# A fused attention and mixture-of-experts kernel: the last tile's outputs normalised on ScalarE, three low parts moved one step, the job table read elsewhere

## The chip, the core and the metric

The kernel runs on one core of a Trainium2 chip. The metric is device time in microseconds (us), the median of several executions; lower is better. Durations of single instructions come from one profiled execution.

## The reference, cut to what matters

```python
B, H, S, D = 8, 8, 576, 64                    # batch, heads, sequence, head size
k_p, v_p = k.reshape(B, H, 72, 8, D).mean(3), v.reshape(B, H, 72, 8, D).mean(3)
scores = (1 / np.sqrt(D)) * np.matmul(q, k_p.transpose(0, 1, 3, 2))
attn = np.exp(scores - scores.max(-1, keepdims=True))
attn = attn / (attn.sum(-1, keepdims=True) + 1e-9)
x = np.matmul(attn, v_p).transpose(0, 2, 1, 3).reshape(4608, 512)
logits = x @ w_gate                           # 8 experts
e_idx = logits.argmax(1)
probs = softmax(logits)
eom = 1 / (1 + np.exp(-(x @ w_output_gate)))
for e in range(8):                            # each row goes to one expert
    mask = e_idx == e
    h = np.maximum(x[mask] @ w1[e], 0)        # 512 -> 1024
    out[mask] = gate_w[mask, None] * eom[mask, e, None] * (h @ w2[e])
```

## The kernel before, in words

The program has two stages with a barrier between them (the profile puts the barrier down to L1716, the line that opens the first stage's scheduling context).

**Stage one** is `attention_and_routing`, written as one order of instructions per engine; each engine follows its own order and waits on semaphores. It walks over 36 tiles of 128 rows in a software pipeline: at step i, in two halves a = 0 and 1, it computes the scores of tile i (`scores`, L279), the peak (`peak`, L285, VectorE), the exponentials (`softmax`, L291, ScalarE), the transposes of tile i-2 (`transpose_p`, L304) and the output of tile i-3 (`values`, L313: matmuls; L330: VectorE's reciprocals of the row sums into `grec`). `normalise` (L333 to L338) then multiplies the unnormalised outputs, 3 heads in half 0 and 5 heads in half 1, by those reciprocals: one VectorE `tensor_tensor` per half (L336) that reads PSUM and writes `xg` in a layout where the 8 heads lie side by side, so that neighbouring elements of one head are 8 floats apart. Each head has 80 columns: 16 gate logits and 64 outputs. The last tile is i = 35; its two PSUM tiles are named `av`.

`route(g)` is a generator that routes four tiles at a time: L352 (`lg`, the sum of the gate logits over heads, which needs all heads of the four tiles), then a chain of small VectorE operations (mx L356, d L358, cand L362, best L364, oh L366), two exponentials on ScalarE (ex L359, ez L373), the rank matmuls (`rk`, L376 and L378) on the matmul engine PE, and the destination `where` (L401), with which GpSimd scatters the rows to DRAM (L447). After the last group, `closing` and `job_table` (L414 to L437, L705 to L735) count the rows of each expert and write `table`, ten integers.

The first expert's first 384 rows are taken early: `turn_x` (L483) transposes them on VectorE (part 0, L486), rounds them to the high part on ScalarE (part 1, L488) and takes the low part on VectorE (part 2, L490), at steps that `TURNS` lists for the three row blocks.

After the loop over tiles a hand-written string `TAIL` orders the rest. Each letter calls `first_layer`: M is a chunk of the first layer (L669, 12 matmuls; the first M has two chunks, 24 matmuls, and takes all products with high parts first), H its ReLU on ScalarE (L525), L its low part on VectorE (L529), a, A the splitting of weights on ScalarE (L475), d, D that on VectorE (L479), W n takes n pieces from the queue of routing generators, R computes slot rows on VectorE (L692 to L702), Y is three matmuls of the second layer (L675), and T makes each of the five engines read the ten integers of `table` into registers (L516, `TENSOR_LOAD`). Below, L0 to L7 are the eight low parts and D0 to D3 the four split pieces of VectorE in this order.

**Stage two** is `experts`: every engine loops over experts by the register values of the job table, with semaphores written out by hand. PE first runs the remaining 33 second-layer matmuls of the first block (L675), then the next products (L1105, L1130).

Of the kernel before, what the change touches and what calls it, by code (L numbers as in the profile page):

```python
# [15 lines left out]
AF = mybir.ActivationFunctionType  # L16
# [4 lines left out]
B, H, S, D = 8, 8, 576, 64  # L21
KEYS, POOL = 72, 8
N, DM, FF, E = B * S, H * D, 1024, 8
P = 128
NT = N // P
# [5 lines left out]
R = 56  # L31
# [5 lines left out]
GATE = 2 * E  # L37
LEAD = GATE * H
# [7 lines left out]
HEADS = (3, 5)  # L46
# [11 lines left out]

TAIL = 'M a W9 d H L W3 M A H L W6 D M A H L W6 D M A H L W6 D M A H L W12 D M H L R M H L T Y Y Y Y Y H L'.split()
F0 = TAIL.count('Y')

AHEAD = {3: 8, 2: 8}
# [1 line left out]
INIT = 5  # L66
POS = (4, 6)
BEHIND = 2
TURNS = ((35.5, 36, 36), (36, 37, 37), (37, 37, 37))
AHEAD_OF_X = 8  # L70
HALF = 512
PARITY = 29120
# [22 lines left out]
def attention_and_routing(ctx, tc, sh, qT, kT, v, wg, wst, xs):  # L95
    nc = tc.nc
# [174 lines left out]
    s_t, pT_t, xg, grec = {}, {}, {}, {}  # L271
# [34 lines left out]
    def values(i, a):  # L306
        av = sh.p_y[a] if i < NT - 1 else ps_t.tile([P, 512], F32, tag="t", name=f"av{a}")
        pT = pT_t[i]
        slot = 4 * a
        for c in chunks(a):  # L310
            _, h, n_heads = CHUNKS[c]
            for r0, n, b, s0 in segments(i):
                nc.tensor.matmul(av[r0:r0 + n, COLS * h:COLS * (h + n_heads)], pT[:, c, r0:r0 + n],  # L313
                                 vbd[b % 2][:, slot:slot + n_heads].rearrange("p h f -> p (h f)"),
                                 start=(c == chunks(a)[0]), stop=(c == chunks(a)[-1]), skip_group_check=True)
            slot += n_heads
        g, j = place[i]
        if a == 0:
            if j == 0:
                while len(placed) < sum(GROUPS[:max(g - 2, 0)]):  # L320
                    work(1, True)
                    place_ids()
                xg[g] = p2.tile([P, GMAX, LEAD + ROW], F32, tag="xg", name=f"xg{g}", bufs=3)
                n, t0 = group(g)
                nc.gpsimd.iota(xg[g][:, 0:n, LEAD + ID:], pattern=[[P, n], [0, ROW - ID]], base=t0 * P, channel_multiplier=1,
                               allow_small_or_imprecise_dtypes=True)
                grec[g] = p2.tile([P, GMAX, H], F32, tag="grec", name=f"grec{g}")
        hs = slice(3 * a, 3 + 5 * a)
        avv = av[:, 0:HEADS[a] * COLS].rearrange("p (h f) -> p h f", h=HEADS[a])
        nc.vector.reciprocal(grec[g][:, j, hs], avv[:, :, COLS - 1])  # L330
        return avv

    def normalise(i, a, avv):  # L333
        g, j = place[i]
        hs = slice(3 * a, 3 + 5 * a)
        nc.vector.tensor_tensor(xg[g][:, j, 0:LEAD + DM].rearrange("p (f h) -> p f h", h=H)[:, :, hs],  # L336
                                avv[:, :, 0:GATE + D].rearrange("p h f -> p f h"),
                                grec[g][:, j, hs].unsqueeze(1).to_broadcast([P, GATE + D, HEADS[a]]), op=ALU.mult)  # L338
# [134 lines left out]
    def split_hi(c, whole=0):  # L473
        m, h, src, hi, lo = early(c, whole)
        nc.scalar.activation(hi, src, AF.Copy)  # L475

    def split_lo(c, whole=0):
        m, h, src, hi, lo = early(c, whole)
        nc.vector.tensor_tensor(lo, src, hi.bitcast(F32), op=ALU.subtract)  # L479
        if h and m + STAGES < LOADED:  # L480
            stage_in(m + STAGES)
# [12 lines left out]
    def first_layer(kind):  # L494
        if kind == "M":
            accs = {}
            for _ in range(1 if layered else 2):
                f = len(layered)
                accs[f] = (sh.p_h + sh.p_y[1:])[f % 4][:, 0:WIDE * P]
                layered.append(accs[f])  # L500
            hidden_chunks(nc, sh, accs)
        elif kind == "Y":
            outputs.append(output_chunk(nc, sh, len(outputs), sh.p_y[0], 0))
        elif kind == "a":
            split_hi(AHEAD_OF_X - 1)
        elif kind == "d":
            split_lo(AHEAD_OF_X - 1)
        elif kind == "A":
            split_piece.append(len(split_piece))
            split_hi(2 * 4 + split_piece[-1], 1)  # L510
        elif kind == "D":
            split_lo(2 * 4 + split_done.pop(), 1)
        elif kind == "T":
            assert not queue
            for eng in (nc.tensor, nc.scalar, nc.vector, nc.gpsimd, nc.sync):
                sh.loaded[eng.engine] = nc.values_load_multi_w_load_instructions(  # L516
                    sh.table[0:1, 0:E + 2], [eng.engine], min_val=0, max_val=1023,
                    skip_runtime_bounds_check_because="counts of a few bits each")[1]
        elif kind == "R":
            slot_rows(lambda ins: None, nc.vector, sh, past_rows(sh, 0, 2 * WIDE), line_rows(sh, 0, 2 * WIDE), sh.number[:, 0:2 * WIDE],  # L520
                      sh.base[:, :, 0:2 * WIDE], sh.ids[:, 0:2 * WIDE], sh.at[:, 0:2 * WIDE])
        elif kind == "H":
            f = len(high)
            high.append(f)
            nc.scalar.activation(sh.ht[:, 0, f], layered[f], AF.Relu)  # L525
        else:
            f = len(low)
            low.append(f)
            nc.vector.scalar_tensor_tensor(sh.ht[:, 1, f], layered[f], 0.0, sh.ht[:, 0, f].bitcast(F32),  # L529
                                           op0=ALU.max, op1=ALU.subtract)  # L530
# [3 lines left out]
    def at(step, f, *args):  # L534
        plan.setdefault(step, []).append((f, args))
# [23 lines left out]
    for b in range(1, B):  # L559
        f = S * b // P + 0.5 * (b % 2)  # L560
# [22 lines left out]
    at(33, gather_early)  # L583
    for part, steps in enumerate(TURNS):
        for k, step in enumerate(steps):
# [21 lines left out]
    for i in range(NT + 3):  # L607
        for a in range(2):
            if i < NT:
                scores(i, a)  # L610
            avv = None
# [10 lines left out]
            if 0 <= i - 3 < NT:  # L622
                avv = values(i - 3, a)
# [14 lines left out]
    for step in sorted(x for x in plan if x > NT + 2):  # L638
        for f, args in plan[step]:
            f(*args)  # L640
    for step in TAIL:
        if step[0] == "W":
            for _ in range(int(step[1:])):
                work(1, True)
                while todo:
                    place_ids()
        else:
            first_layer(step)
# [13 lines left out]
def hidden_chunks(nc, sh, accs):  # L662
    terms = [(f, d, part, x) for f in accs for d in range(4) for part, x in ((0, 0), (0, 1), (1, 0))]
    if 0 in accs:
        terms.sort(key=lambda term: term[3])
    seen = {f: 0 for f in accs}
    for f, d, part, x in terms:
        o = DM * f + P * d
        nc.tensor.matmul(accs[f], sh.first_w[0][:, part, o:o + P], sh.xt[:, x, d, :], start=(seen[f] == 0), stop=(seen[f] == 11))  # L669
        seen[f] += 1  # L670


def output_chunk(nc, sh, f, acc, k):
    for part, h in ((0, 0), (1, 0), (0, 1)):
        i = nc.tensor.matmul(acc, sh.ht[:, h, f, P * k:P * k + P], sh.first_w[1][:, part, DM * f:DM * f + DM],  # L675
                             start=(f == 0 and part == 0 and h == 0), stop=(f == 7 and h == 1), skip_group_check=True)
    return i


def past_rows(sh, c0, c1):  # L680
    o = WIDE * ROW
    return sh.rows[:, o:o + 2 * (E - 1) * R].rearrange("p (c e r) -> p c e r", c=2, e=E - 1)[:, :, :, c0:c1]


def line_rows(sh, c0, c1):
    o = WIDE * ROW + 2 * (E - 1) * R
    return sh.rows[:, o:o + 2 * R].rearrange("p (c r) -> p c r", c=2)[:, :, c0:c1]


def slot_rows(done, v_, sh, past, line, number, base, rows, at):  # L690
    n = number.shape[-1]
    done(v_.tensor_tensor(past[:, 0], number.unsqueeze(1).to_broadcast([P, E - 1, n]),  # L692
                          sh.upto[:, 0:E - 1].unsqueeze(2).to_broadcast([P, E - 1, n]), op=ALU.is_ge))
    for c in (1, 0):
        ins = v_.tensor_tensor(past[:, c], past[:, 0], sh.skip[:, c].unsqueeze(2).to_broadcast([P, E - 1, n]), op=ALU.mult)
    done(ins)
    done(v_.tensor_reduce(line, past.rearrange("p c e r -> p c r e"), axis=AX.X, op=ALU.add))
    done(v_.tensor_tensor(line, line, base, op=ALU.add))
    done(v_.tensor_tensor(line[:, 1], line[:, 0], line[:, 1], op=ALU.is_lt))
    done(v_.scalar_tensor_tensor(line[:, 0], line[:, 0], float(-ZROW), line[:, 1], op0=ALU.add, op1=ALU.mult))  # L700
    v_.tensor_scalar(at, line[:, 0], float(ZROW), None, op0=ALU.add)
    done(v_.tensor_scalar(rows, line[:, 0], float(PARTS), float(PARTS * ZROW + PARTS - 1), op0=ALU.mult, op1=ALU.add))  # L702
# [1048 lines left out]
```

## Time and profile before

| | |
|---|---|
| median of 3 runs | 587.99 us (587.48 to 588.24) |
| the profiled execution | 588.69 us |
| its span, first to last instruction | 586.9 us |
| granted clock of TensorE | 1.000 over the span |
| busy: PE, DVE, ACT, POOL | 96%, 61%, 44%, 38% of the span |

In the profile, PE is the matmul engine and PEld its weight load, DVE is VectorE, ACT is ScalarE, POOL is GpSimd, SP is SyncE; a name with q is that engine's sequencer. A row of a timeline gives the start, the duration, engine, line, operation, the written and read tiles, the shape and the number of instructions that the row merges; in brackets stands the idle time before it and what ended it. Where a row merges several instructions its duration runs from the first start to the last end; neighbouring instructions of one engine overlap in part, so that the next one's start says when the engine was free for it.

### The profile page before, as it was taken

What the parts mean: (1) busy time and instruction counts of PE and PEld (TensorE: products, weight loads), DVE (VectorE), ACT (ScalarE), POOL (GpSimd) and SP (SyncE); (2) the same over time, 40 slices, a digit from 0 to 9 for tenths busy, and PEclk for the clock granted to TensorE, in tenths of its full rate; (3) what the DMA queues carried; (4) which work ended last, traced back from release to release, by engine and by line L of the source; (5) the groups of instructions that cost most, each with busy time, mean ns of one, the idle gap of its engine ahead of it and who ended that gap; (6) DMA issues with size and microseconds to landing.
All of it is one profiled execution on the core that took longest, in us unless ns stands there. A gap on an engine that the chain in (4) does not pass through costs nothing.

```text
span 586.9 us, 12639 instructions
## 1 busy us (share of the span) xinstructions
PE 562.9 (96%) x3347; PEld 509.6 (87%) x3347; DVE 356.9 (61%) x865; ACT 258.5 (44%) x703; POOL 224.2 (38%) x331
## 2 busy tenths in 40 slices
PE   2999999999999999999999999999999999999996
PEld 1799898888988989798989898998998898989895
DVE  6789999988978723768385723428436741322322
ACT  2889888889524404446264421217123520202120
POOL 2878888940735423154313141230212422213131
PEclk9999999999999999999999999999999999999999
DMA  9858979976557730476555733214615212020110
GB/s 335 291 233 326 353 289 359 346 298 175 187 191 194 286 92 22 129 246 164 226 167 190 241 128 89 47 45 116 236 27 153 59 35 71 2 71 20 40 33 36
DMA packets 44075, 96.08 MB, mean 164 GB/s; under 512 B 5451, under 2 KB 27899, under 8 KB 41088
## 3 DMA queue, kind: packets, MB, share of 16 engines
q1 hardware_dynamic: 28752, 48.69, 25.9%
q10 hardware_dynamic: 7488, 27.27, 13.3%
q0 software_dynamic: 7792, 19.61, 9.2%
q8 instruction: 19, 0.31, 0.2%
q14 instruction: 24, 0.20, 0.1%
HBM read 76.10 MB, written 22.91 MB: 169 GB/s over the span
## 4 chain that ended last, share of the span: by engine, by line
PE 70%; issue 0%; POOL 0%; DVE 0%; ACT 0%; POOLq 0%
PE p_h L1130 33%; PE p_y L1105 33%; PE p_y L1116 1%; PE p_y L675 1%; PE p_h L1141 1%; PE p_h L1150 0%; POOL out L1645 0%; DVE rows L1448 0%; ACT q_even L1278 0%; PE p_y L1185 0%; POOLq L845 0%; POOLq L807 0%; POOLq L1612 0%
## 5 line engine op out<-in xcount | busy, mean ns | idle before, releaser
L1130 PE MATMUL p_h<-xt,all_weights 128*128 128x384 f32 (+1 forms) x1056 | 164.7, 316 | 0.0
L1130 PEld LDWEIGHTS p_h<-xt,all_weights 128*128 128x128 f32 x1056 | 163.2, 189 | 1.7 <-issue 0.9
L1105 PE MATMUL p_y<-all_weights,ht 128*128 128x512 f32 x696 | 159.9, 390 | 0.0
L1105 PEld LDWEIGHTS p_y<-all_weights,ht 128*128 128x128 f32 x696 | 130.3, 188 | 26.6
L1267 ACT ACTIVATE ht<-p_h 128x384 fp32r<-128x384 f32 (+1 forms) x104 | 46.1, 450 | 221.8 <-PE p_h L1130 206.3
L1645 POOL DMA_INDIRECT out<-rows,dst x41 | 42.1, 1028 | 215.1 <-DVE rows L1448 207.8
L1456 DVE SCALAR_TENSOR_TENSOR ht<-p_h,ht 128x384 fp32r<-128x384 f32 (+1 forms) x104 | 51.7, 504 | 99.7 <-ACT ht L1267 91.7
L291 ACT ACTIVATE p<-p_h,m 128x72 f32<-128x72 f32 x288 | 69.9, 348 | 15.4 <-DVE m L285 15.1
L1448 DVE TENSOR_SCALAR rows<-p_y,sc 128x512 f32<-128x512 f32 x39 | 28.7, 749 | 76.2 <-PE p_y L1105 66.5
L313 PE MATMUL p_y<-vbd,pT 128*128 128x162 f32 (+3 forms) x390 | 67.0, 320 | 2.6 <-DVE xg L336 2.1
L1620 POOL DMA_INDIRECT rows<-xs,src x51 | 59.1, 1160 | 24.9 <-POOL src L1616 14.5
L1522 DVE TENSOR_TENSOR all_weights<-all_stages,all_weights x44 | 52.3, 1222 | 13.9 <-ACT all_weights L1333 13.5
L313 PEld LDWEIGHTS p_y<-vbd,pT 128*128 128x128 f32 (+1 forms) x390 | 52.7, 179 | 7.1 <-ACT pT L304 2.0
L1333 ACT ACTIVATE all_weights<-all_stages x44 | 44.6, 1052 | 16.9 <-PE p_y L1105 14.2
L447 POOL DMA_INDIRECT xs<-xg,where x36 | 37.5, 1042 | 35.6 <-DVE grec L330 28.0
L205 POOL TENSOR_TENSOR kq<-kq 128x288 f32<-128x288 f32 (+1 forms) x63 | 42.7, 685 | 18.0 <-DMA kq<-kT 14.7
L279 PE MATMUL p_h<-kbd,q_even 128*128 128x144 f32 (+1 forms) x160 | 29.1, 310 | 11.6 <-DMA q_even<-qT 8.9
L1247 ACT ACTIVATE xt<-turned 128x512 fp32r<-128x512 f32 x40 | 24.1, 626 | 29.1 <-DVE turned L1391 28.0
L279 PEld LDWEIGHTS p_h<-kbd,q_even 128*128 128x128 f32 (+1 forms) x160 | 23.1, 193 | 14.0 <-issue 9.7
L336 DVE TENSOR_TENSOR xg<-p_y,grec 128x240 f32<-128x240 f32 x70 | 34.4, 491 | 1.3
L285 DVE TENSOR_REDUCE m<-p_h 128x4 f32<-128x288 f32 x72 | 32.3, 449 | 3.5 <-PE p_h L279 2.9
L1105 PE MATMUL p_y<-w2a,ht 128*128 128x512 f32 x144 | 33.2, 390 | 0.0
(180 smaller groups left out, 648.6 us busy)
## 6 DMA issues: line engine op xcount, KB each, us to landing
all_stages<-wst ACTq DMA_DIRECT2D x52, 512.0 KB
rows<-v SPq DMA_DIRECT2D x8, 1280.0 KB, 6.4
kq<-kT SPq DMA_DIRECT2D x7, 1152.0 KB, 11.3
rows<-xs SPq DMA_DIRECT2D x36, 192.0 KB, 4.8
all_stages<-wst SPq DMA_DIRECT2D x12, 512.0 KB, 9.1
kq<-qT SPq DMA_DIRECT2D x4, 1152.0 KB, 8.7
q_even<-qT SPq DMA_DIRECT2D x3, 1152.0 KB
rows<-xs SPq DMA_DIRECT2D x20, 128.0 KB
```

What stands on the lines that cost most here:

```text
L205: eng.tensor_tensor(k[:, :, 0:w], k[:, :, 0:w], k[:, :, w:2 * w], op=ALU.add)
L279: nc.tensor.matmul(s[r0:r0 + n, 144 * c:144 * c + 144], q_t[b][:, 2 * a + c, s0:s0 + n], kbd[b % 2][:, 2 * a + c, :], start=True, stop=True)
L291: nc.scalar.activation(pt[i % 3][:, o:o + KEYS], sv[:, h], AF.Exp, bias=m[:, h:h + 1])
L313: nc.tensor.matmul(av[r0:r0 + n, COLS * h:COLS * (h + n_heads)], pT[:, c, r0:r0 + n], vbd[b % 2][:, slot:slot + n_heads].rearrange("p h f ...
L1105: i = mm(to, ht[:, h, f, P * k:P * k + P], w[:, part, o:o + DM], start=(f == 0 and part == 0 and h == 0), stop=(f == 7 and h == 1))
L1130: i = mm(p_h[f % DEEP][:, 0:n], w[:, part, o:o + P], xt[:, x, d, 0:n], start=(d == 0 and part == 0 and x == 0), stop=(d == 3 and part == 1))
L1267: act(ht[:, 0, f, 0:n], p_h[f % DEEP][:, 0:n], AF.Relu).then_inc(q["hh"], 1)
L1333: act(hi, s, AF.Copy).then_inc(q["wh"], 1)
L1456: nc.vector.scalar_tensor_tensor(ht[:, 1, f, 0:n], src, 0.0, ht[:, 0, f, 0:n].bitcast(F32), op0=ALU.max, op1=ALU.subtract).then_inc(q["hl" ...
L1522: nc.vector.tensor_tensor(lo, s, hi.bitcast(F32), op=ALU.subtract).then_inc(q["wl"], 1)
L1620: nc.gpsimd.indirect_dma_start(out=xm[:, k].bitcast(I32), out_offset=None, in_=xs, in_offset=bass.IndirectOffsetOnAxis(ap=src[:, k:k + 1], ...
L1645: nc.gpsimd.indirect_dma_start(out=out, out_offset=bass.IndirectOffsetOnAxis(ap=dst[:, k:k + 1], axis=0), in_=yb[2 if k == size - 1 else k ...
```

## The change

The letter V is new: VectorE alone reads the job table there, and T is now for the other four engines, after the third Y. The third entry of `TURNS` moves the low parts (L490) of all three blocks from step 37 to step 38, that is, from behind the half in which tile 34 is finished to behind the half in which tile 35 is. For the last tile `normalise` issues one ScalarE activation per head, three in half 0 and five in half 1, each a copy of 80 columns with the head's reciprocal as the scale of each partition.

```diff
-TAIL = 'M a W9 d H L W3 M A H L W6 D M A H L W6 D M A H L W6 D M A H L W12 D M H L R M H L T Y Y Y Y Y H L'.split()
+TAIL = 'M a W9 d H L W3 M A H L W6 D M A H L W6 D M A H L W6 D V M A H L W12 D M H L R M H L Y Y Y T Y Y H L'.split()
...
-TURNS = ((35.5, 36, 36), (36, 37, 37), (37, 37, 37))
+TURNS = ((35.5, 36, 36), (36, 37, 37), (38, 38, 38))
...
     def normalise(i, a, avv):
         g, j = place[i]
         hs = slice(3 * a, 3 + 5 * a)
+        if i == NT - 1:
+            rows = xg[g][:, j, 0:LEAD + DM].rearrange("p (f h) -> p f h", h=H)
+            for h in range(HEADS[a]):
+                nc.scalar.activation(rows[:, :, 3 * a + h], avv[:, h, 0:GATE + D], AF.Copy, scale=grec[g][:, j, 3 * a + h:3 * a + h + 1])
+            return
         nc.vector.tensor_tensor(xg[g][:, j, 0:LEAD + DM].rearrange("p (f h) -> p f h", h=H)[:, :, hs],
...
-        elif kind == "T":
+        elif kind in "VT":
             assert not queue
-            for eng in (nc.tensor, nc.scalar, nc.vector, nc.gpsimd, nc.sync):
+            for eng in (nc.vector,) if kind == "V" else (nc.tensor, nc.scalar, nc.gpsimd, nc.sync):
                 sh.loaded[eng.engine] = nc.values_load_multi_w_load_instructions(
```

## Rows read from the trace of the kernel before

**Rows 1.** The page, part 1: busy time of each engine.
```profile
PE 562.9 (96%) x3347; PEld 509.6 (87%) x3347; DVE 356.9 (61%) x865; ACT 258.5 (44%) x703; POOL 224.2 (38%) x331
```

**Rows 2.** The timeline of PE, 146 to 200 us.
```profile
148.87 1.68 PE L313 MATMUL av<-vbd,pT 128*128 128x162 f32 x10
150.28 4.45 PE L669 MATMUL p_h<-xt,w1a 128*128 128x384 f32 x24
155.48 0.18 PE L376 MATMUL rk<-oh,tri 128*128 128x40 bf16 x1 [0.76 <-DVE oh L367]
...
159.88 6.40 PE L669 MATMUL p_h<-xt,w1a 128*128 128x384 f32 x36
...
168.20 3.60 PE L675 MATMUL p_y<-w2a,ht 128*128 128x512 f32 x15
172.93 7.76 PE L675 MATMUL p_y<-w2a,ht 128*128 128x512 f32 x33 [1.13 <-PEq L1716]
```

**Rows 3.** The timeline of DVE, 146 to 168 us: around the last tile.
```profile
150.43 1.89 DVE L490 TENSOR_TENSOR xt<-rows,xt 128x512 fp32r<-128x512 f32 x3
152.23 0.18 DVE L330 RECIPROCAL grec<-av 128x3 f32<-128x3 f32 x1
...
152.45 0.41 DVE L336 TENSOR_TENSOR xg<-av,grec 128x240 f32<-128x240 f32 x1
...
152.99 0.58 DVE L336 TENSOR_TENSOR xg<-av,grec 128x400 f32<-128x400 f32 x1
153.60 0.69 DVE L352 TENSOR_REDUCE lg<-xg 128x64 f32<-128x512 f32 x1
```

**Rows 4.** The sources of the barrier: line L1716, count, min/median/max ns, first and last start.
```profile
L1716 PEldq DRAIN  x2: 13/2068/4123, 167.7 to 172.3; - x2
...
L1716 DVEq DRAIN  x2: 19/286/553, 171.4 to 172.3; - x2
```

**Rows 5.** The timeline of ACT, 146 to 200 us: around the last tile.
```profile
149.58 0.61 ACT L475 ACTIVATE w1a<-all_stages 128x512 fp32r<-128x512 f32 x1
154.77 0.23 ACT L359 ACTIVATE ex<-d 128x32 f32<-128x32 f32 x1 [4.58 <-DVE d L358]
```

**Rows 6.** The timeline of ACT, 20 to 40 us: runs of short activations.
```profile
31.57 0.74 ACT L242 ACTIVATE vbd<-vp,mask 128x128 f32<-128x128 f32 x2
...
33.33 0.89 ACT L245 ACTIVATE vbd<-vp,mask 128x64 f32<-128x64 f32 x3
```

**Rows 7.** The groups of ACT by line and form: busy us, mean ns of one.
```profile
L242 ACT ACTIVATE vbd<-vp,mask 128x128 f32<-128x128 f32 x32 | 11.4, 428 | 0.0
L245 ACT ACTIVATE vbd<-vp,mask 128x64 f32<-128x64 f32 x24 | 6.9, 387 | 0.0
```

**Rows 8.** The sources of the table reads: line L516, count, min/median/max ns, start.
```profile
L516 SPq TENSOR_LOAD <-table x1: 2020/2020/2020, 165.3 to 165.3; - x1
...
L516 PEldq TENSOR_LOAD <-table x1: 2107/2107/2107, 165.3 to 165.3; - x1
L516 ACTq TENSOR_LOAD <-table x1: 1522/1522/1522, 166.3 to 166.3; - x1
L516 DVEq TENSOR_LOAD <-table x1: 1308/1308/1308, 170.0 to 170.0; - x1
```

**Rows 9.** The timeline of DVE, 164 to 172 us: from the table to the last low part.
```profile
165.08 0.16 DVE L735 SCALAR_TENSOR_TENSOR table<-jobs 128x7 int32<-128x7 f32 x1
165.15 1.22 DVE L479 TENSOR_TENSOR w2a<-all_stages,w2a 128x1024 fp32r<-128x1024 f32 x1
166.28 0.55 DVE L529 SCALAR_TENSOR_TENSOR ht<-p_h,ht 128x384 fp32r<-128x384 f32 x1
166.75 1.22 DVE L479 TENSOR_TENSOR w2a<-all_stages,w2a 128x1024 fp32r<-128x1024 f32 x1
...
170.16 0.55 DVE L529 SCALAR_TENSOR_TENSOR ht<-p_h,ht 128x384 fp32r<-128x384 f32 x1
171.38 0.56 DVE L529 SCALAR_TENSOR_TENSOR ht<-p_y,ht 128x384 fp32r<-128x384 f32 x1 [0.67 <-issue]
```

## The prediction

> **What bounds the kernel now.** I read the page first: PE is busy for 562.9 of the 586.9 us [rows 1]. So an edit is worth what it takes out of PE's idle time. Next I read PE's timeline over the stretch that the diff touches, and looked for bracketed idle times. There are two [rows 2]. At 155.48 PE has waited 0.76 us for `oh` (L367), the one-hot result of the last routing group. At 172.93 it has waited 1.13 us at the barrier of L1716. All else there is matmuls back to back, one per 0.173 us: the 36 of 6.40 us give (6.40 - 0.33) / 35, with 0.33 us for the last one's own length.
>
> For the first wait I followed VectorE back from `oh`. The chain that makes it begins with L352 at 153.60, and VectorE works without a break before that: three low parts from 150.43 (1.89 us), then a reciprocal and the end of an older group from 152.23, a normalisation at 152.45, the second reciprocal, the second normalisation at 152.99 [rows 3]. The outputs that it normalises have left PE by 150.55 (148.87 + 1.68) [rows 2]. ScalarE meanwhile has nothing after a weight split at 149.58 of 0.61 us: its next activation starts at 154.77 after 4.58 us of idle time [rows 5]. So the first wait is VectorE's queue and nothing else.
>
> For the barrier I read its drains [rows 4]: PE's ends at 167.7 + 4.12 = 171.82, VectorE's at 171.4 + 0.55 = 171.97. VectorE is the last by 0.15 us, and PE restarts 0.96 us after it. VectorE is late because its own table read of 1.31 us [rows 8] leaves it idle for 0.67 us ahead of L7, which starts at 171.38 [rows 9].
>
> **The change part by part.** The sums are against the profiled execution, 588.69 us for a span of 586.9; the median is 0.70 below it. About 0.2%, 1.18 us, is what a measurement of this kernel can tell from no change.
>
> *Low parts behind the reciprocals.* VectorE is free at 150.43. The first reciprocal goes there; the group of three up to 152.45 takes 0.22 us [rows 3], so the second reciprocal follows at 150.65, when its matmuls are done (150.55). The low parts then take 1.89 us from about 150.75 and end at 152.64. PE needs them after the 16 products with high parts only: 150.28 + 16 x 0.173 = 153.05. They are 0.4 us early, and that is the cover: the move costs nothing, and if they came later than 153.05, PE would wait by the excess.
>
> *Eight activations in place of two VectorE operations.* This takes 0.41 + 0.58 us from VectorE [rows 3]. No row shows a ScalarE activation from PSUM into columns 8 floats apart. The nearest rows have the same scale per partition and contiguous columns: three of 64 columns in 0.89 us, each 0.387 long, so one starts 0.25 after the other; two of 128 in 0.74, each 0.428, so 0.31 [rows 6, 7]. For 80 columns I take 0.26. The first can start when the first reciprocal is written, 150.43 + 0.18 = 150.61, say 150.65; the second reciprocal is there before the fourth. The eighth starts at 150.65 + 7 x 0.26 = 152.47 and ends 0.40 later, at 152.87. L352 then starts at about 152.91 instead of 153.60, because low parts end at 152.64 and no longer decide. Gain of the chain: **0.69 us**. The split that stood at 149.58 now comes behind the activations and ends by 153.6; VectorE's half of it (d) follows the routing chain, after 155, so this costs nothing. The bounds: VectorE's low parts allow L352 no earlier than 152.68, a gain of 0.92; the other end is ScalarE at twice 0.26 an activation, 152.47 + 1.82 + 0.44 = 154.73, a loss of 1.13. I take 0.69, as the scale per partition and the column count are those of the rows, and only the step of the write is not. A row bears on that step from the other engine: VectorE writes this layout 240 elements in 0.41 and 400 in 0.58 us [rows 3], 1.06 ns for each further element, so the step alone did not hold VectorE up.
>
> [...]
>
> PE: the rank matmuls come 0.69 earlier, at 154.79, which is after the end of the first chunk's matmuls at 154.73, so PE gains the whole 0.69. Its last Y drains at 171.82 - 0.69 = 171.13. The chunks of M that wait for a free accumulator don't bind; their low parts move by as much.
>
> *V: VectorE's table read behind D2.* The table is written at 165.08 + 0.16 = 165.24, D2 runs from 165.15, and L4 stands right behind the read [rows 9]. In the old time frame the read begins at 165.26. Its price is not known: VectorE's own read, alone, took 1.31 us; the three reads that began at 165.3 took 2.02 to 2.11; ScalarE's, begun beside them, 1.52 [rows 8]. With 1.31, L4 starts at 165.26 + 1.31 + 0.05 = 166.62 instead of 166.28, 0.34 later; with 2.05, 1.08 later. I take 0.34: the engine is the same, and ScalarE's read was not drawn up to 2. Queued behind L4 are D3, L5, the slot rows and L6, all back to back, so the delay runs to the barrier; PE's Y4 needs L4 only some 3 us later, so nothing else waits.
>
> *No table read ahead of L7.* Two VectorE instructions of which the first is a low part start 0.47 apart (166.28, 166.75), so L7 could start at 170.16 + 0.47 = 170.63 instead of 171.38 [rows 9]: **0.75** saved. ScalarE's H7 that it needs comes well before.
>
> *T behind the third Y.* On PE the read now stands behind nine queued matmuls, which run to about 169.5 in the new frame (167.51 + 9 x 0.23), while the table is ready at about 164.5. Even 2.11 us of read, begun as late as 166, ends before these nine do; without that cover PE would pause for the read's rest. For ScalarE, GpSimd and SyncE neither place nor time of T changes but for the common shift; no DMA is issued or moved past.
>
> *Sum.* VectorE drains at 171.97 - 0.69 + 0.34 - 0.75 = 170.87, PE at 171.13. PE is late next: the barrier's last arrival moves from 171.97 to 171.13, **0.84 us**. Behind it, stage two starts from the barrier on every engine and PE has no long wait in it that another clock sets, so the shift lasts to the end: 588.69 - 0.84 = 587.85, and for the median 587.99 - 0.84 = **587.1 us**.
>
> **The rivals.**
> *Slow table read* (0.25): three engines start their reads together, as SyncE, GpSimd and PE did; VectorE now replaces PE among them. V then costs 1.08, VectorE drains at 171.97 - 0.69 + 1.08 - 0.75 = 171.61 and is again last: gain 0.36, 587.6 us. For it: the three simultaneous reads [rows 8]. Against: ScalarE's 1.52.
> [...]
>
> *ScalarE is the new late one* (0.10, the other side): the eight activations take over from VectorE as what L352 waits for. From 0.36 us apart (153.60 - 0.44 - 150.65 over 7) the chain is later than before; at 0.52 PE's rank matmuls come 1.13 later, PE drains at 172.95 and the kernel takes 0.98 us more, 589.0. For it: the unseen write step. Against: VectorE's rows on it.
>
> *Everything as early as it can be* (0.12): activations 0.22 apart, so that the low parts decide: PE gains 0.92, the barrier 1.07: 586.9.
>
> *Inert* (0.08): the gain ahead of the barrier is real, but a transfer in stage two that doesn't move with the barrier takes it back: 588.0. PE's unbroken rows behind 172.93 speak against it.
>
> **How the numbers follow.** The forecast's own case has 0.45. The runs of before spread by 0.38 to either side of their middle, so a case of 587.1 or 586.9 may be read as over 0.2% faster now and then: 0.07 from the forecast, 0.08 from the early case, together 0.16 with a little for the unseen. Over 0.2% slower needs activations 0.55 apart or more, or a rearranged instruction stream that I can't see: 0.09. The rest, 0.75, is within 0.2%. The range goes from 586.9 less the spread, 586.5, up to 588.5, which takes in the slow read, the inert case and the milder half of the slow ScalarE.
>
> **What would show it.** Right: eight ScalarE activations about 0.26 apart from 150.65; L352 at 152.9; PE's wait for `oh` at or below 0.1 us; VectorE's read near 1.3 us behind the table; the barrier's last drain PE's, near 171.1. Wrong: the activations more than 0.36 apart, PE pausing inside its first 24 matmuls for the low parts, VectorE's drain still last, or the time after the barrier being longer than the 414 us (586.9 - 172.9) that it is now.

## The result, and the profile after

The changed kernel takes 591.07 us (median of 8 runs, 589.62 to 593.24) against 588.00 (587.04 to 589.04, 8 runs) for the kernel before, measured beside it: a ratio of 1.0054, 95% interval 1.0038 to 1.0070. It is slower by some 3 us, where 0.84 us less was forecast, and the range of 586.5 to 588.5 does not hold it. The profiled execution took 590.02 us for a span of 588.3; three of the eight runs had a mean granted clock of 1.000 and took 589.6 to 590.5 us, the five at 0.997 and 0.998 took 590.6 to 593.2. Line numbers of the changed kernel are 5 above those of before.

I cut the span where TensorE (PE) shows a seam: the first matmul of M after the attention; PE's restart behind the barrier; the first matmul of the last part, L1130 before and L1135 after. The view is the busy time by stretches: length, then busy time of PE, PEld, DVE, ACT and POOL with counts, then the granted clock, the DMA share and GB/s. Of the kernel before:

```profile
150.28:172.93 22.65, 20.76 (x118) 19.59 (x118) 20.15 (x83) 7.77 (x14) 11.12 (x10) 1.00 0.59 199
172.93:185.97 13.04, 13.04 (x57) 10.78 (x58) 10.32 (x18) 5.27 (x7) 6.39 (x10) 1.00 0.65 160
185.97:586.90 400.93, 395.25 (x2163) 358.51 (x2161) 197.56 (x287) 123.05 (x204) 108.33 (x148) 1.00 0.36 112
```

And of the changed kernel:

```profile
148.78:171.08 22.30, 20.62 (x119) 19.52 (x118) 19.32 (x81) 10.15 (x23) 10.22 (x10) 1.00 0.59 202
171.08:187.07 15.99, 13.16 (x58) 10.60 (x58) 10.05 (x18) 5.00 (x7) 7.38 (x11) 1.00 0.52 123
187.07:588.20 401.13, 395.44 (x2162) 358.59 (x2162) 197.89 (x287) 123.68 (x204) 104.30 (x148) 1.00 0.37 113
```

The stretch that the change edits is 0.35 us shorter (22.65 to 22.30). The next, in which no line was changed, is 2.95 us longer (13.04 to 15.99). The rest is 0.2 longer. The first matmul of M itself comes 1.50 us earlier in this one execution, with the same program ahead of it; in the other profiles below it comes anywhere from 149.3 to 152.5 with no order in it, so I count from there.

The changed stretch on PE, then the waits of PE (engine, tile, line and releaser: us in total, times, longest):

```profile
148.78 4.44 PE L674 MATMUL p_h<-xt,w1a 128*128 128x384 f32 x24
153.08 0.18 PE L381 MATMUL rk<-oh,tri 128*128 128x40 bf16 x1
...
165.79 3.60 PE L680 MATMUL p_y<-w2a,ht 128*128 128x512 f32 x15
171.08 7.73 PE L680 MATMUL p_y<-w2a,ht 128*128 128x512 f32 x33 [1.68 <-PEq L1721]
178.64 5.60 PE L1110 MATMUL p_y<-w2a,ht 128*128 128x512 f32 x24
187.07 4.26 PE L1135 MATMUL p_h<-xt,w1a 128*128 128x384 f32 x23 [2.83 <-DVE xt L1392]
```

```profile
PE p_h L1135 <- DVE xt L1392: 2.8, 1, 2.8
PE p_y L680 <- PEq L1721: 1.7, 1, 1.7
```

Against [rows 2], the wait for `oh` is gone: the rank matmul comes 4.30 us after the first M instead of 5.20. The wait at the barrier is longer, 1.68 for 1.13. And there is a wait that did not exist before, 2.83 us for `xt` ahead of L1135. That wait is the loss.

ScalarE (ACT) and VectorE (DVE) around the last tile, in their timelines, answering to [rows 3, 5]:

```profile
149.15 1.95 ACT L339 ACTIVATE xg<-av,grec 128x80 f32<-128x80 f32 x8 [0.97 <-DVE grec L330]
150.84 0.69 ACT L480 ACTIVATE w1a<-all_stages 128x512 fp32r<-128x512 f32 x1
```

```profile
149.17 0.18 DVE L330 RECIPROCAL grec<-av 128x5 f32<-128x5 f32 x1
149.28 1.85 DVE L495 TENSOR_TENSOR xt<-rows,xt 128x512 fp32r<-128x512 f32 x3
151.13 0.69 DVE L357 TENSOR_REDUCE lg<-xg 128x64 f32<-128x512 f32 x1
...
162.67 0.16 DVE L740 SCALAR_TENSOR_TENSOR table<-jobs 128x7 int32<-128x7 f32 x1
162.75 1.22 DVE L484 TENSOR_TENSOR w2a<-all_stages,w2a 128x1024 fp32r<-128x1024 f32 x1
165.18 0.56 DVE L534 SCALAR_TENSOR_TENSOR ht<-p_h,ht 128x384 fp32r<-128x384 f32 x1 [1.22 <-ACT ht L530]
...
169.07 0.55 DVE L534 SCALAR_TENSOR_TENSOR ht<-p_h,ht 128x384 fp32r<-128x384 f32 x1
169.54 0.55 DVE L534 SCALAR_TENSOR_TENSOR ht<-p_y,ht 128x384 fp32r<-128x384 f32 x1
```

The table reads, L521, and the barrier's drains, L1721 (count, min/median/max ns, first and last start), answering to [rows 4, 8]:

```profile
L521 SPq TENSOR_LOAD <-table x1: 2163/2163/2163, 162.9 to 162.9; - x1
L521 POOLq TENSOR_LOAD <-table x1: 2232/2232/2232, 162.9 to 162.9; - x1
L521 DVEq TENSOR_LOAD <-table x1: 2268/2268/2268, 162.9 to 162.9; - x1
...
L521 PEldq TENSOR_LOAD <-table x1: 1277/1277/1277, 164.3 to 164.3; - x1
```

```profile
L1721 PEldq DRAIN  x2: 13/1820/3628, 165.8 to 170.4; - x2
...
L1721 DVEq DRAIN  x2: 19/600/1180, 168.9 to 170.4; - x2
```

VectorE's read started with two others and took 2.27 us; L4 stood behind it with 1.22 us of idle time, and VectorE drained at 168.9 + 1.18 = 170.1, still later than PE (165.8 + 3.63 = 169.4).

Now behind the barrier. ScalarE's first two weight loads of the stage, in its timeline, before and after:

```profile
172.75 0.89 ACTq L1251 DMA_DIRECT2D all_stages<-wst  x2
```

```profile
171.50 2.73 ACTq L1256 DMA_DIRECT2D all_stages<-wst  x2
```

The single durations are 0.41 and 0.45 us before, 2.25 and 0.44 after: issuing the first load took 1.84 us more. What moves in those 2.3 us, by DMA queue (packets, MB, share of 16 engines), from 172.75 in the kernel before and from 171.50 in the changed one:

```profile
q10 hardware_dynamic: 61, 0.25, 52.4%
```

```profile
DMA packets 1, 0.01 MB, mean 4 GB/s; under 512 B 0, under 2 KB 0, under 8 KB 0
...
q14 instruction: 1, 0.01, 0.9%
```

Queue 10 carries the weights. In the changed kernel none of them moves; one packet does, of 8192 bytes, on an instruction queue, 0.69 us after the load's start. Before, the packet of that queue comes at 176.78, after both loads. I take this packet to be ScalarE's code. The queue has other 8192-byte packets too, but one series goes by ScalarE's count: a packet comes behind 61, 189, 316, 447 and 570 of the ScalarE instructions in the trace of the kernel before, and behind 62, 189, 317, 444 and 568 in that of the changed one, so 123 to 131 apart, and this packet is the last of these. That it moves when instructions are added to ScalarE alone is shown by the experiments.

The end of the chain is VectorE's, before and after:

```profile
181.96 1.92 DVE L1391 STREAM_TRANSPOSE turned<-rows 128x512 f32<-128x512 f32 x3 [1.41 <-DMA rows<-xs]
183.78 1.87 DVE L1387 TENSOR_TENSOR xt<-turned,xt 128x512 fp32r<-128x512 f32 x3
```

```profile
183.34 1.91 DVE L1396 STREAM_TRANSPOSE turned<-rows 128x512 f32<-128x512 f32 x3 [4.64 <-DMA rows<-xs]
185.16 1.85 DVE L1392 TENSOR_TENSOR xt<-turned,xt 128x512 fp32r<-128x512 f32 x3
```

The rows of the first jobs (SyncE's transfer `rows<-xs`) reach VectorE 9.03 us after PE's restart before, 12.26 after. SyncE doesn't issue them later: its first transfer stands at 175.56 before and at 173.70 after, 2.63 and 2.62 us behind the restart. What differs is what moves beside them. Before, the packets of the rows' queue q1 run from 3.93 to 8.20 us behind the restart and those of the two weight loads end at 4.47; after, the rows run from 5.14 to 11.63 and the weights end at 7.81. PE takes the last low part when it is made: 185.16 + 1.85 = 187.01, PE at 187.07. Before, they were ready at 183.78 + 1.87 = 185.65 for a matmul at 185.97. So the stretch that looked unbroken had 0.32 us to spare.

### The profile page after: what moved, and what is told of

It reads as the page before. It is cut to its first block, busy times and chain, and to the rows that moved or that the text cites. A ratio compares the mean times of both kernels' runs of the same rounds, so it can differ in the third digit from the quotient of the medians.

```text
span 588.3 us, 12650 instructions
## 1 busy us (share of the span) xinstructions
PE 563.7 (96%) x3347; PEld 510.4 (87%) x3347; DVE 355.9 (61%) x863; ACT 260.9 (44%) x711; POOL 220.6 (37%) x331
## 4 chain that ended last, share of the span: by engine, by line
PE 67%; DMA 1%; issue 1%; SPq 1%; DVE 0%; POOL 0%; ACT 0%; DVEq 0%; POOLq 0%
PE p_h L1135 33%; PE p_y L1110 32%; PE p_y L1121 1%; DMA rows<-xs 1%; PE p_h L1146 1%; PE p_h L1155 0%; SPq L1067 0%; DVE xt L1392 0%; POOL out L1650 0%; DVE rows L1453 0%; ACT q_even L1283 0%; PE p_y L1190 0%; DVE turned L1396 0%; SPq L1061 0%; SPq L1040 0%
## 5 line engine op out<-in xcount | busy, mean ns | idle before, releaser
L1135 PE MATMUL p_h<-xt,all_weights 128*128 128x384 f32 (+1 forms) x1056 | 164.8, 316 | 0.1
L1135 PEld LDWEIGHTS p_h<-xt,all_weights 128*128 128x128 f32 x1056 | 163.2, 189 | 1.8 <-issue 0.9
L1625 POOL DMA_INDIRECT rows<-xs,src x51 | 56.9, 1115 | 25.0 <-POOL src L1621 14.7
L1396 DVE STREAM_TRANSPOSE turned<-rows 128x512 f32<-128x512 f32 x42 | 27.6, 695 | 10.2 <-issue 5.5
```

What stands on the lines that cost most here:

```text
L1135: i = mm(p_h[f % DEEP][:, 0:n], w[:, part, o:o + P], xt[:, x, d, 0:n], start=(d == 0 and part == 0 and x == 0), stop=(d == 3 and part == 1))
L1625: nc.gpsimd.indirect_dma_start(out=xm[:, k].bitcast(I32), out_offset=None, in_=xs, in_offset=bass.IndirectOffsetOnAxis(ap=src[:, k:k + 1], ...
```

## The experiments

**Theory**: the twelve instructions that the change adds to ScalarE (eight activations and four semaphore waits on the same line) move its code so that a code packet is due just at the first weight load behind the barrier; the load is issued 1.8 us late, the weights then share the DMA engines with the rows, and the rows come late. **Rivals**: the new order of VectorE and the table reads does it; extra ScalarE work costs by itself; the late weights matter otherwise. The extra activations below copy one column of zeros to a scratch tile that nothing reads. Line numbers in these kernels are up to four higher. The kernel before, run beside them, took 589.50 us (587.98 to 594.70) on the chip of the first four kernels that were run (twelve added, the first with sixteen, and the two halves), and 588.38 and 587.76 us on another chip, beside the rest; a ratio is the recorded comparison with it, not the quotient of two medians.

**Twelve activations in the kernel before, nothing else.**

```
             nc.scalar.activation(sh.ht[:, 0, f], layered[f], AF.Relu)
+            for _ in range({4: 4, 5: 4, 6: 4}.get(f, 0)):
+                nc.scalar.activation(spare[:, len(filled):len(filled) + 1], zeros[:, 0:1], AF.Copy)
+                filled.append(f)
```

> The kernel before with nothing of the change, but with 12 one-column activations on a scratch tile in ScalarE's idle time of the tail (four each behind H4, H5 and H6), so that its instruction stream up to the barrier is as much longer as in the changed kernel (eight activations and four semaphore waits). Theory 'code position': a block of ScalarE's code is fetched at one place of its stream, which now falls on the two weight loads behind the barrier; they start some 2 us late, run into the row transfer, and PE waits. Expected: 590 to 591.5 us, PE's wait ahead of the first L1130 2 to 3.5 us, the first weight load's issue 1.5 to 2.5 us long, an 8 KB packet of queue 14 within 2 us of the barrier. Rival 'new order' (the earlier barrier, the table reads or the moved work bring the late transfer): 588.0, no wait there.

It took 594.86 us, ratio 1.0092 (1.0057 to 1.0127), above the expected 590 to 591.5. Its stretch ahead of the barrier is as before (22.7 us), its first weight load took 2.23 us with the code packet 0.68 behind its start, and the stretch behind the barrier grew:

```profile
174.99:191.56 16.57, 13.21 (x58) 10.60 (x58) 10.04 (x18) 5.00 (x7) 7.30 (x11) 1.00 0.53 118
191.56:196.00 4.44, 4.44 (x16) 4.44 (x17) 4.33 (x5) 2.14 (x4) 1.59 (x2) 0.62 1.05 327
```

The loss appears with nothing of the change but its count. The second row adds a cost of its own: behind a wait of 3.4 us PE's clock was granted at 0.62 on average over 4.44 us. I had not counted that cost in the expectation.

**Twenty-eight in the kernel before.** The same edit with {4: 9, 5: 9, 6: 10}.

> The kernel before with 28 one-column activations (12 made it 5.4 us slower, ratio 1.0092). Code position theory: 28 is what the changed kernel with 16 has added in all (8 activations and 4 waits with them), so the code fetch comes ahead of the barrier and the loss is gone: the first weight load in 0.4 us, restart to the first matmul of the last phase 13.0 us, 587.8 to 588.9 us, ratio 0.9995 to 1.0015. Rival (the extra activations cost by their own time): more than twice the loss of 12, ratio above 1.01.

Measured: 587.92 us, ratio 1.0003 (0.9992 to 1.0015). More than twice the work, and no loss:

```profile
171.98:185.01 13.03, 13.03 (x57) 10.77 (x58) 10.68 (x18) 5.64 (x8) 6.64 (x10) 1.00 0.67 172
```

The first load took 0.41 us; the code packet had come at 166.39, ahead of the barrier. So it is the place of the code and not the work.

**The changed kernel with sixteen more** ({4: 5, 5: 5, 6: 6}; 28 added in all), and the same again.

> The changed kernel with 16 more one-column activations on a scratch tile in ScalarE's idle time of the tail (five behind H4, five behind H5, six behind H6). Code position: the fetch falls ahead of the barrier, where ScalarE waits anyway; the loads start at the barrier as before; 587.3 to 588.0 us, since the gain ahead of the barrier (0.35 us by the traces) is all that is left; no wait of PE over 0.3 us at the first L1130. New order: 590 to 592, the wait of 2.8 us stays.

> The same kernel as the one with 16 one-column activations added behind the changed kernel's ScalarE work (on a scratch tile, extra work only), run again because its first profile had TensorE's semaphores arrive late in the first stage. Code position theory: the first weight load of ScalarE behind the barrier is issued in about 0.4 us, not 2.2; no wait ahead of the first L1139; restart to first L1139 is 13.0 us; against the kernel before the change's gain of about 0.35 us ahead of the barrier remains, less what 16 more activations cost (0 to 0.3): ratio 0.9990 to 1.0005. Rival, that the change loses for another reason (clock, contention): ratio 1.004 to 1.007 as for the change itself.

The first one showed the load back at 0.41 us and 13.04 us behind the barrier, but 592.72 us, ratio 1.0068 (1.0045 to 1.0091): its profile has another disturbance, ahead of the barrier, where ScalarE waited 3.51 us, up to 158.24, for a semaphore of PE whose matmuls were done by 154.28, and that stretch was 25.69 us long. The same kernel on another chip took 588.18 us, ratio 1.0000 (0.9989 to 1.0012):

```profile
149.27:171.40 22.13, 20.59 (x118) 19.49 (x118) 19.30 (x81) 11.60 (x39) 10.23 (x10) 1.00 0.61 204
171.40:184.40 13.00, 13.00 (x57) 10.78 (x58) 10.55 (x18) 5.51 (x7) 6.53 (x11) 1.00 0.66 166
```

So the change's loss goes with the place of the code, and what is left is its gain ahead of the barrier, 0.52 us here, too small to be told from nothing.

**Half of the change at a time**: the new TAIL alone, and the new normalisation and low parts with the old TAIL.

> Only the new TAIL (VectorE's table read at V, the other four at the new T); the last tile stays on VectorE and the low parts at step 37. ScalarE's stream is as long as before. Code position: no late loads; 587.9 to 588.6 us, as VectorE's read in the middle of its queue costs about 1.0 us and saves 0.75 at the end. New order, in the form that the table reads bring the late transfer: 590 to 591.5.

> The new normalisation on ScalarE and the moved low parts, with the old TAIL. Code position: ScalarE's stream is 12 longer, so the loads are late as in the changed kernel: 589.3 to 591, with a barrier about 0.9 us earlier and a wait of PE of 2 to 3.5 us behind it. New order, with the table reads at fault: 587.0 to 587.3, no wait behind the barrier.

TAIL alone adds nothing to ScalarE's code: 590.56 us, ratio 1.0016 (0.9989 to 1.0042), above the expected 587.9 to 588.6, the two first loads 0.89 us together as in the kernel before, no wait at L1135. Its profiled execution had PE's semaphores late as well, then a 2.98 us wait at the barrier and a clock of 0.57 in the 6.9 us behind it, so its size says little. The normalisation alone, which adds the twelve instructions: 595.34 us, ratio 1.0103 (1.0075 to 1.0131), the wait at L1135 1.9 us, 15.12 us behind the barrier, and in the first 3.0 us of these only one packet of 8192 bytes moves; it too had the late semaphores (25.21 us ahead of the barrier), so 595.34, above the expected range as well, overstates it. TAIL alone can't be told from no change and the normalisation alone is slower, as the theory has it; the sizes are inconclusive.

**Weights held back until the rows are in**, in the changed kernel.

```
         rows = table(eng)
+        eng.wait_ge(q["xd"], 2 * LANDED)
         for m in range(LOADED, STAGES + EARLY):
             load(m)
```

> The changed kernel, with one wait added on ScalarE: its weight loads of the last stage start only when the row transfer has landed (some 4.2 us behind the last row transfer's issue), so the two no longer move at the same time. If the 2.83 us wait ahead of L1135 comes from weight loads and row transfer sharing the DMA engines, the rows come in time, that wait shrinks below 0.5 us and the stretch from TensorE's restart to the first L1135 is near 13.0 to 13.5 us, although the weights are now even later; a wait for weights may show further on. If it comes from something else (the late instructions alone, VectorE's own queue), the wait stays within 2 to 3.5 us. In the first case the kernel takes 587.5 to 588.5 us where the later weights are hidden, in the second 590 to 592.

593.69 us, ratio 1.0105 (1.0083 to 1.0128), and a wait of 3.81 us at L1135: by the letter of the expectation the link is something else. But the trace says why. From 8.05 us after PE's restart on, until 184, the rows' queue q1, which carries 1600 packets in all, moved this much in the kernel before and in the changed one:

```profile
q1 hardware_dynamic: 7, 0.00, 0.5%
```

```profile
q1 hardware_dynamic: 919, 0.45, 53.9%
```

With the weights held back the same view has no q1 at all; all its 1600 packets lie ahead of that, although the code packet came at 173.41, 1.1 us behind the restart:

```profile
q10 hardware_dynamic: 166, 0.63, 55.4%
q0 software_dynamic: 2, 0.00, 0.2%
```

Without weights beside them the rows are in time (by 8.05 us behind the restart, for 8.20 before and 11.63 in the changed kernel), so I put their lateness down to sharing the DMA engines. PE waits nonetheless because VectorE's part of the weight split stands ahead of its work on the rows:

```profile
183.32 2.36 DVE L1434 TENSOR_TENSOR all_weights<-all_stages,all_weights 128x1024 fp32r<-128x1024 f32 x2 [5.88 <-ACT all_weights L1263]
```

I had not looked at that order when I wrote that the later weights might show only further on.

**The parts that gain, without the loss.** Both kernels have the normalisation, the low parts and the sixteen activations; in the first all five engines read the table behind the third Y, in the second VectorE's read V stands behind D3 instead of D2.

TAIL from its third D on is, in the changed kernel, in the first and in the second:

```
D V M A H L W12 D M H L R M H L Y Y Y T Y Y H L
D M A H L W12 D M H L R M H L Y Y Y T Y Y H L
D M A H L W12 D V M H L R M H L Y Y Y T Y Y H L
```

> The change's normalisation on ScalarE and its order of the low parts, with the 16 one-column activations that move ScalarE's code, but one table read by all five engines together behind the third Y (VectorE's too, none behind D2). Theory (code position, and a table read of 2.2 us for VectorE behind D2 as what held the barrier): the barrier's last drain is TensorE's or VectorE's near 171.0 to 171.3, TensorE restarts 0.7 to 1.0 us earlier than before, restart to the first matmul of the last phase stays 13.0 us: 587.0 to 587.4 us, ratio 0.9983 to 0.9990. Rival (the read behind the third Y holds VectorE ahead of L7 as before, or ScalarE's code again late): 588 to 590.

> As the kernel with one read by all five engines, but VectorE's read of the table stands behind D3, later than the other engines would start theirs behind the third Y or beside them. If a read alone takes 1.3 us and one that starts with two others 2.2, it costs VectorE 1.3 us here at a place where it has to wait little, and the barrier is bound by TensorE: first M to restart 21.6 to 21.8 us (22.65 before, 22.30 in the changed kernel), the whole 586.8 to 587.3 us. Rival: the read still overlaps the others' and takes 2 us or more, VectorE drains last, first M to restart 22.2 to 22.6, the whole 587.5 to 588.

One read: 587.27 us, ratio 0.9984 (0.9968 to 1.0000), first M to restart 21.74 us. V behind D3: 586.71 us, **ratio 0.9974 (0.9964 to 0.9984)**, faster than the kernel before and the changed one; the intervals of the two new kernels overlap, so V's place between them is judged by the traces (21.74 and 21.58 us) and not by the times:

```profile
149.46:171.04 21.58, 20.59 (x118) 19.49 (x118) 19.21 (x81) 11.60 (x39) 10.22 (x10) 1.00 0.62 209
171.04:184.07 13.03, 13.03 (x58) 10.73 (x59) 10.18 (x18) 5.14 (x7) 6.59 (x10) 1.00 0.64 155
```

My reason for it was wrong in one point: the read didn't wait for the others to be done and take 1.3 us. It began with them at 163.5 and took 2.15 us, though it stands behind L4 and D3 in the program:

```profile
163.41 1.22 DVE L485 TENSOR_TENSOR w2a<-all_stages,w2a 128x1024 fp32r<-128x1024 f32 x1
164.55 0.55 DVE L538 SCALAR_TENSOR_TENSOR ht<-p_h,ht 128x384 fp32r<-128x384 f32 x1
165.02 1.21 DVE L485 TENSOR_TENSOR w2a<-all_stages,w2a 128x1024 fp32r<-128x1024 f32 x1
166.15 0.55 DVE L538 SCALAR_TENSOR_TENSOR ht<-p_h,ht 128x384 fp32r<-128x384 f32 x1
```

```profile
L522 DVEq TENSOR_LOAD <-table x1: 2152/2152/2152, 163.5 to 163.5; - x1
```

The read is made while the arithmetic issued ahead of it still runs, and ended at 165.69, before D3 (165.02 + 1.21) did. Behind D2 only D2 itself covers it, and 1.22 us were left over; behind D3 there is no idle time.

**Eight and none of the sixteen**, in that best kernel: 20 and 12 instructions added.

> The kernel with VectorE's read behind D3, with 8 one-column activations in place of 16. Code position theory: what counts is that ScalarE's 8 KB code fetch comes before the barrier, where ScalarE waits anyway, and eight instructions put it there as well: the first weight load is issued in 0.4 us, restart to the first L1139 is 13.0 us, no wait ahead of it: 586.5 to 587.2 us, ratio 0.9965 to 0.9985 as with 16. Rival (it takes 16, or their delay and not their place counts): a wait of 2 to 3 us ahead of L1139, 588.5 to 590.

> The same kernel with none of these activations: ScalarE's code is placed as in the changed kernel itself. Code position theory: the first weight load takes some 2.2 us again, with an 8 KB code packet about 0.7 us behind its start, and TensorE waits 2 to 3.5 us ahead of the first L1135; first M to restart stays near 21.6 us: 588.8 to 590.2 us, ratio 1.001 to 1.004. Rival (VectorE's read, not ScalarE's code, made the changed kernel slow): no such wait, 586.5 to 587.2.

With none: 590.44 us, ratio 1.0040 (1.0019 to 1.0062), first load 2.30 us, 15.74 us behind the barrier: the wait and the late load as expected (the time is 0.24 us above the expected range), and against the rival, since VectorE's read is harmless here. With eight: 591.28 us, ratio 1.0063 (1.0045 to 1.0081), where I had expected the full gain. The first load took 2.21 us, with the code packet at 171.75, 0.66 us into it:

```profile
170.99:186.66 15.67, 13.19 (x57) 10.59 (x57) 10.04 (x18) 5.00 (x7) 6.88 (x11) 1.00 0.52 127
186.66:191.00 4.34, 4.34 (x16) 4.34 (x17) 4.33 (x5) 2.19 (x4) 1.59 (x2) 0.62 1.05 300
```

Eight are not enough: the load still meets the packet. That miss narrows the place: of the undisturbed kernels, those with 0 or 28 added instructions issue the first load in 0.41 us and need 13.00 to 13.04 us behind the barrier; those with 12 or 20 (the one with the held-back weights apart) need 2.2 to 2.3 us and 15.67 to 16.57.

## Why the prediction was wrong

**Low parts behind the reciprocals: right.** They run from 149.28 to 151.13, and PE's first 24 matmuls have no gap (4.44 us against 4.45).

**Eight activations: right, a little under-counted.** The first starts 0.37 us after the first M, as forecast. They are (150.6 - 149.15) / 7 = 0.21 apart, not 0.26, and end by 151.10; the low parts decide after all, as in the rival "everything as early as it can be". The chain gained 5.20 - 4.30 = 0.90 us for the 0.69 forecast. The write step, which no row had shown for ScalarE, cost nothing that shows: the strided 80 columns start closer together, 0.21 us, than the contiguous 64 of [rows 6], 0.25 us, which read another tile (`vp`).

**V: the wrong row was taken.** I took 1.31 us from VectorE's lone read; started beside SyncE's and GpSimd's it took 2.27. L4 comes 16.40 us after the first M for 16.00 before, and with the 0.90 gained ahead of it V cost 1.30, not 0.34. That is the rival "slow table read", with 1.08 worked out from 2.05. ScalarE's and PE's reads, which began 1.0 and 1.4 us behind the three, took 1.51 and 1.28.

**No read ahead of L7: right.** L6 and L7 start 0.47 apart (169.07, 169.54) instead of 1.22: 0.75.

**T behind the third Y: right.** PE's read took 1.28 us beside matmuls that have no gap.

**The sum ahead of the barrier**: 0.90 - 1.30 + 0.75 = 0.35, which is what the stretch shows; 0.84 was forecast, 0.36 under the rival. That the rival's 0.36 comes so near is luck: it had the chain's gain 0.21 too small (0.69 for 0.90) and the price of V 0.22 too small (1.08 for 1.30), and the two cancel.

**The step that failed** is the sentence after the sum: "stage two starts from the barrier on every engine and PE has no long wait in it that another clock sets, so the shift lasts to the end". It rested on PE's rows being unbroken behind 172.93. The prediction's own sign of being wrong came: the time from the restart to the end grew from 414.0 to 417.1 us (588.2 - 171.08). The unbroken rows show that nothing was late, not how little was missing: VectorE finished `xt` 0.32 us before PE took it, behind a wait of its own for the rows of 1.41 us. A 1.84 us delay of one load on ScalarE's queue was enough. I named "a rearranged instruction stream that I can't see" for the slower tail only, as one part of 0.09, and gave it no place and no price. The trace of before could have given the place: it shows the packet 3.6 us behind the second of those loads (176.78 against 173.19), and the change added twelve instructions to the engine that issues them. It could not have given the price, since neither of those two loads meets a packet in it.

**What makes 3 us of it**: 2.95 behind the barrier and 0.2 after it, less the 0.35 gained, is 2.8 in the profiled execution. Its wait of 2.83 us left the clock at 1.00. In the profiles of four other kernels with this wait (2.48 to 3.81 us) the clock fell to 0.61 to 0.64 behind it, and the part from there to the end was 1.6 to 1.8 us longer than in the nearest kernel without that fall (with eight activations 4.34 + 398.50 = 402.84, with none 4.43 + 398.30 = 402.73, against 401.03 with sixteen in the same kernel). So these executions paid for the wait twice; that this makes the spread of the changed kernel's runs agrees with their clocks but was not shown.

**Open**: the late semaphores of PE in three profiles of one chip, which no edit here explains, and what exactly holds the load for 2.2 us where the packet comes: the trace has packets and no addresses. In the kernel before a packet of the same queue at 184.56 lies in a pair of weight loads (183.92, 0.84 us) that it does not stretch. By its place I take it for VectorE's and not ScalarE's: such a packet comes behind 697 instructions of VectorE before and behind 698 in the changed kernel (at 188.72), but behind 582 and 598 of ScalarE.

## What to carry to other kernels

Before an edit that adds or removes instructions on an engine, look where that engine's code packets fall and what it issues first behind a barrier: if the two can meet, price the meeting (here 2.25 us for a load of 0.41), and try the edit with some idle instructions more before judging it (here eight were not enough and sixteen were). An unbroken row on the bounding engine says nothing about slack; read how long before its use the last operand was made (here 0.32 us). Put a register read behind arithmetic that is already issued, where it runs beside it (2.15 us without idle time behind D3), rather than ahead of arithmetic that has to wait for it (1.22 us of idle time behind D2).

## What the runs showed of the hardware

- The first weight load that ScalarE issues behind the barrier took 2.21 to 2.25 us in place of 0.41 in three kernels in which a packet of 8192 bytes came 0.66 to 0.69 us behind its start (the changed one, the one before with twelve activations, the best one with eight); it took 0.41 where the packet came 4.03 us behind its start (before) or ahead of the barrier (before with twenty-eight, changed with sixteen).
- Three engines that began to read the same ten words together took 1.94 to 2.27 us each (three profiles); ScalarE's and TensorE's, begun 1 us or more behind them, 1.20 to 1.52, and VectorE's lone one 1.31 (two profiles).
- VectorE's register read overlapped with arithmetic issued before it: 2.15 us left no idle time behind D3 in the best kernel.
- ScalarE wrote 80 fp32 columns from PSUM on a step of 32 bytes at 0.21 us an activation, each 0.42 to 0.46 long.
- In tail_only's profile, a 2.98 us wait of PE at the barrier was followed by 6.9 us at a granted clock of 0.57.
